# Loading x ahead of the weights, and a last product with buffers of its own, in a four-layer attention kernel

## The chip, the cores and the metric

The kernel runs on one core of one Trainium2 chip. The metric is the device time of one execution in microseconds (us), as the median of several runs. The engines are named as in the profile: PE (TensorE, matrix products), DVE (VectorE), ACT (ScalarE), POOL (GpSimd) and SP (SyncE, which here only issues transfers).

## What is computed

A residual stream x of 2048 tokens by 640 features passes through four layers, A, B, A, B. Each layer adds its result for the layer-normalised x.

```python
x = A_x
x = x + _A_ref(_layernorm(x), A_wq, A_wk, A_wv, A_wo, A_beta)
x = x + _B_ref(_layernorm(x), B_mem0, B_Wq, B_Wk, B_Wv, B_Wo, B_seg_len)
x = x + _A_ref(_layernorm(x), A_wq, A_wk, A_wv, A_wo, A_beta)
x = x + _B_ref(_layernorm(x), B_mem0, B_Wq, B_Wk, B_Wv, B_Wo, B_seg_len)
```

Layer A has 32 heads of 20 features. It cuts the tokens into four segments of 512; within a segment it computes causal softmax attention, and mixes it by a gate per head with a linear-attention read of a state that the earlier segments have filled:

```python
for s in range(4):
    p = softmax(qs @ ks.T * scale + mask);  a_dot = p @ vs
    a_mem = (phi(qs) @ M) / (phi(qs) @ z + 1e-6)
    o = g * a_mem + (1 - g) * a_dot
    M += phi(ks).T @ vs;  z += phi(ks).sum()
return concat(o) @ wo
```

Layer B has 32 heads of 128 features and is recurrent. It makes 64 steps over segments of 32 tokens. In each step 8 memory rows stand ahead of the 32 tokens; the attention's result for these 8 rows is the memory of the next step, and that for the 32 tokens is the output.

```python
for s in range(64):
    h = concat([mem, x[32 * s:32 * s + 32]])
    o = attention(h @ Wq, h @ Wk, h @ Wv, mask) @ Wo
    mem, out[s] = o[:8], o[8:]
```

## The kernel before, in words

The residual stream lies in DRAM (`xres`, float32, with a bfloat16 copy). A layer reads its rows from there and writes them back. Only the first layer reads the input, and only the last writes the output.

**Layer A** (`layer_A`, L161). Each segment is four tiles of 128 tokens. `seg_load` (L220) loads an x tile, `a_xt`, from a pool of two buffers and makes its layernorm `a_xn` at once (two statistics steps, an aggregation and an addition on DVE, a power on POOL, the normalisation on DVE; L80 to L87). `seg_tr` (L229) transposes `a_xn` on PE into PSUM and ACT copies it to `a_xnT` (L237), a pool of two buffers. When all four tiles are there, `proj_q` (L276, `a_QP`) and `proj_k` (L295, `a_KP`) multiply with weights of a group of four heads; eight groups make a segment, so a layer has 32 groups. The rest of a group is scores, row maxima on DVE (L375), exponentials on ACT (L410), products, and the state's update. `out_stage_b` adds the output product to x (L261). A's instructions are given to the framework's scheduler, which decides the order on each engine from dependencies, program order and its own estimate of times. Its PSUM is a pool of three double banks (`psx`, banks 0 to 5) and one of two banks (`pg`, banks 6 and 7), which the transposes and `a_QP` use.

`load_A_weights` (L141) is called after the second x tile of a layer. The first time wq and wk go into a staging place (a corner of B's resident weights), loaded at the very beginning of the program (L1090), and from there DVE copies the 20 columns of each head to a place of 32 (L148), whose other 12 POOL sets to zero (L147). The padded form is kept in DRAM, and the second A layer loads it directly (L150).

**Layer B** (`layer_B`, L543). Here the order on each of PE, ACT, DVE and POOL is the program's own (`_OrdNC`); SP's transfers are not tied. A step gives `b_OPS`, the output of 24 tokens and the memory rows. The product for the last 8 tokens of four consecutive steps is deferred: their attention results are collected in `b_OTdef` and multiplied during the next four steps (`od_chunk`, a quarter at a time) into the PSUM tile `b_OPSd`. `od_begin` (L849) starts one, and `od_end` (L845) adds it to `b_XOd`, the tile with the matching rows of x, and stores it. The next product then needs `b_XOd` loaded anew (`tail_dma`, L822) and the PSUM tile back. After step 63 the deferred product of steps 60 to 63 is still to be done, all four quarters in a row (L1072 to L1074). B's PSUM is a pool of five banks and one with a bank each for the tags `tail`, `ops` and `opsd`.

Of the kernel before, what the change touches and what calls it, by code (L numbers as in the profile page):

```python
# [18 lines left out]
F32 = mybir.dt.float32  # L19
BF16 = mybir.dt.bfloat16  # L20
# [8 lines left out]
D = 640  # L29
# [111 lines left out]
def load_A_weights(nc, W, A_wq, A_wk, A_wv, A_wo, padded, stage):  # L141

    first = not padded
    for nm, src, pad in (("wq", A_wq, W.wq), ("wk", A_wk, W.wk)):
        if first:
            raw = stage[nm]
            nc.gpsimd.memset(pad[:, :, :, 20:32], 0.0)  # L147
            nc.vector.tensor_copy(pad[:, :, :, 0:20], raw.rearrange("p c (h d) -> p c h d", d=20))  # L148
        else:
            nc.sync.dma_start(pad[:].rearrange("p c h s -> p (c h s)"), padded[nm])  # L150
    nc.sync.dma_start(W.wv[:], A_wv.rearrange("(c p) n -> p c n", p=128))
    nc.sync.dma_start(W.wo[:], A_wo.rearrange("(c p) n -> p c n", p=128))
# [8 lines left out]
def layer_A(nc, tc, C, W, x_src, x_dst, src_is_bf16, nseg=4, out_bf16=False, xb_dst=None, load_w=None, side_loads=None):  # L161
    SC = 1.0 / math.sqrt(20.0)
    nc_raw = nc
    if A_ORDERED:
        nc = _OrdNC(tc, nc_raw, engines=ORDER_ENGINES)
# [3 lines left out]
    with ExitStack() as ctx:  # L169
# [7 lines left out]
        pxT = pool("a_xnT", 2)  # L177
        pxt = pool("a_xt", 2)
# [7 lines left out]
        wk = pool("a_wk", 2)  # L186
# [31 lines left out]
        SEG = {}  # L218

        def seg_load(n_, tt):  # L220
            d = SEG.setdefault(n_, {"xn": [None] * 4, "oT": [None] * 4, "xr": [None] * 4})
            r0 = n_ * 512 + tt * 128
            xt = pxt.tile([128, 2 * D] if src_is_bf16 else [128, D], BF16 if src_is_bf16 else F32, name="a_xt")
            nc.sync.dma_start(xt[:, 0:D], x_src[r0:r0 + 128, :])
            xn = pxn.tile([128, D], BF16, name="a_xn")
            layernorm_tile(nc, sml, C, xt[:, 0:D], xn[:], "a_ln")
            d["xn"][tt] = xn
# [219 lines left out]

        for tt in range(4):
            seg_load(0, tt)
            if tt == 1:  # L450
                load_w()
            seg_tr(0, tt)
        proj_q(0)
        proj_k(0)
# [1 line left out]
        for g in range(NGR + 2):  # L456
            n, G = divmod(g, 8)
            for half in range(2):
                p = 2 * g + half
                for r in range(3):  # L460
                    if g < NGR:
                        s_round(p, r)
                    if 0 <= p - 3 < 2 * NGR:
                        t_round(p - 3, r)
                    k = (half, r)
                    if k == (0, 0) and g + 1 < NGR:
                        proj_q(g + 1)
                    if k == (0, 1):
                        if 0 <= g - 1 < NGR:
                            q_with_max(g - 1)  # L470
                        if n >= 1 and 2 <= G <= 5 and n <= nseg:
                            out_stage_a(n - 1, G - 2)
                        if n + 1 < nseg and G in (0, 1, 6):
                            seg_load(n + 1, min(G, 2))
                            seg_tr(n + 1, min(G, 2))
                    if k == (0, 2) and g + 1 < NGR:
                        proj_k(g + 1)
                    if k == (1, 0) and g < NGR:
                        proj_v(g)
                    if k == (1, 1):  # L480
                        if 0 <= g - 2 < NGR:
                            pv(g - 2)
                        if g < NGR:
                            phi_k(g)
                    if k == (1, 2):
                        if 0 <= g - 2 < NGR:
                            norm(g - 2)
                        if g < NGR:
                            state(g)
                        if n >= 1 and 2 <= G <= 5 and n <= nseg:  # L490
                            out_stage_b(n - 1, G - 2)
                        if n + 1 < nseg and G == 6:
                            seg_load(n + 1, 3)
                            seg_tr(n + 1, 3)
            if g < NGR:
                negmax_rows(g)
            if side_loads is not None and n == 0:
                if G == 0:
                    build_gates(nc, st, W, side_loads[1])
                side_loads[0](G, GS[g]["kT"])  # L500
# [42 lines left out]
def layer_B(nc, tc, C, W, x_src, xb_src, x_dst, mem0, B_Wv, B_Wo, nsteps=64, out_bf16=False, tag=""):  # L543
# [7 lines left out]
    with ExitStack() as ctx:  # L551
# [291 lines left out]
                    od["n"] = k + 1  # L843

        def od_end():  # L845
            x_out(od["ps"], XOd, lambda xo: tail_dma(od["s0"], True, xo), "d")
            od.clear()

        def od_begin(s0):  # L849
            od.update(s0=s0, n=0, ps=po.tile([128, 320], F32, name="b_OPSd", tag="opsd"))  # L850

        def ln_g(s):
            return 2 * (s // 8) + 4 + (s % 8 == 5)
# [4 lines left out]
        for s in range(nsteps):  # L858
# [200 lines left out]
                vtail_evac(unit[0], unit[1], vps, "act")  # L1059
            if od and od["n"] == 4:  # L1060
                od_end()
                tail_dma(s - 3, False, XOd)
                od_begin(s - 3)
            elif s == 3:
                tail_dma(0, False, XOd)
                od_begin(0)
            x_out(ops, XO, store_head(s), "")
            nc.gpsimd.tensor_copy(OTdef[(s // 4) % 2][:, :, 8 * (s % 4):8 * (s % 4) + 8], OTsb[:].rearrange("p (h c) -> p h c", c=40)[:, :, 0:8])
            if ln_xt_due(s + 1):
# [7 lines left out]
def full_kernel(tc, A_x, A_wq, A_wk, A_wv, A_wo, A_beta, B_x, B_mem0, B_Wq, B_Wk, B_Wv, B_Wo, B_seg_len, out, layers="ABAB"):  # L1077
    nc = tc.nc
    with ExitStack() as ctx:
        C, WA = alloc_consts(tc, ctx)  # L1080
        xin = A_x.rearrange("b s d -> (b s) d")
        xout = out.rearrange("b s d -> (b s) d")
        mem0 = B_mem0.rearrange("b t d -> (b t) d")
        X = tc.dram_tile([S_TOK, D], F32, name="xres")
        Xb = tc.dram_tile([S_TOK, D], BF16, name="xres_bf")
        WB = alloc_B_resident(tc, ctx)
        padded = {}
        stage = {nm: t_[:, NCH - 1, 0:NCH * D].rearrange("p (c n) -> p c n", c=NCH) for nm, t_ in (("wq", WB.wq), ("wk", WB.wk))}
        for nm, src in (("wq", A_wq), ("wk", A_wk)):
            nc.sync.dma_start(stage[nm], src.rearrange("(c p) n -> p c n", p=128))  # L1090
        build_consts(nc, tc, C)
        nl = len(layers)
        assert layers[0] == "A" and layers[-1] == "B"
        for li, L in enumerate(layers):
            lastl = (li == nl - 1)
            if L == "A":
                first = li == 0

                def side(G, after):
                    load_B_resident(nc, WB, B_Wq, B_Wk, G, after)  # L1100
# [66 lines left out]
```

## Time and profile before

| what | us |
|---|---|
| median of three runs | 2835.52 |
| lowest and highest | 2830.86, 2836.12 |
| the profiled execution | 2836.99 |
| its span, first to last instruction | 2835.3 |
| PE busy | 2667.9 (94%) |
| DVE busy | 1676.5 (59%) |
| ACT busy | 1567.3 (55%) |
| POOL busy | 702.8 (25%) |

A row of the timeline gives the start in us from the beginning of the span, the busy time in us, engine, line, operation, output and inputs, and how many instructions are merged (x5). In brackets stands how long the engine was idle before it and what ended that. SPq and ACTq are the queues on which SP and ACT issue transfers; the time there is that of the issue. The chain of waits follows the program back from its last instruction and names at each step what released it. The granted clock is that of TensorE, 1.00 being full speed. Nearly all helpers of layer B record their operations under one line (L105), so its groups are told apart by tile names.

### The profile page before, as it was taken

Reading aid. Unit: us, or ns where it says so; the run is one execution under the profiler, and the core shown is the slowest. Engines: PE = TensorE matmul, PEld = TensorE weight load, DVE = VectorE, ACT = ScalarE, POOL = GpSimd, SP = SyncE. Lnnn points to the kernel's source line nnn. Section 1 sums busy time; section 2 is a strip of 40 time slices with the busy share of each in tenths; the row PEclk is TensorE's granted clock in tenths of the full one; section 3 lists DMA queues with packets and bytes.
Section 4 is the critical chain, followed back from the end, with each engine's and each line's share of the span. In section 5 each row is a group of like instructions: output and inputs, shape, how many; then the busy total and the mean of one; then the engine's idle time right before and its main releaser. Section 6 shows DMA issues by size and latency. Waiting matters only on the chain.

```text
span 2835.3 us, 147285 instructions
## 1 busy us (share of the span) xinstructions
PE 2667.9 (94%) x65736; PEld 1703.8 (60%) x65736; DVE 1676.5 (59%) x4554; ACT 1567.3 (55%) x3516; POOL 702.8 (25%) x1634
## 2 busy tenths in 40 slices
PE   5899998999999999999979999889999999999998
PEld 2455555666666666666635555556666666666665
DVE  5778864555555555555568878545555555555554
ACT  3777773555555555544448777545555555555443
POOL 3456651111111111111135666411111111111110
PEclk9999999999999999999989999899999999999999
DMA  6110135212221222121130111531211111211110
GB/s 215 53 43 23 39 127 134 44 40 47 44 44 42 43 46 45 41 41 31 31 114 20 57 48 34 174 94 41 43 39 41 41 41 42 43 40 38 39 26 20
DMA packets 322956, 156.54 MB, mean 55 GB/s; under 512 B 245776, under 2 KB 311056, under 8 KB 319248
## 3 DMA queue, kind: packets, MB, share of 16 engines
q1 hardware_dynamic: 320880, 136.63, 19.1%
q8 instruction: 514, 8.42, 1.3%
q10 hardware_dynamic: 1440, 10.49, 1.0%
q14 instruction: 122, 1.00, 0.1%
HBM read 95.65 MB, written 51.38 MB: 52 GB/s over the span
## 4 chain that ended last, share of the span: by engine, by line
PE 54%; DVE 4%; ACT 3%; DMA 2%; issue 1%; POOL 1%; SPq 0%; ACTq 0%; DVEq 0%; POOLq 0%
PE b_OPS L105 7%; PE b_tail L105 4%; PE b_Ka L105 4%; PE b_Qa L105 4%; PE b_Kb L105 4%; PE b_Qb L105 4%; PE b_Va L105 3%; PE b_Vb L105 3%; PE b_SP L105 3%; PE b_OTP L105 2%; PE b_PTP L105 2%; PE b_vtail L105 2%; PE b_OPSd L105 2%; DVE a_nm L375 2%; PE a_QP L276 1%
## 5 line engine op out<-in xcount | busy, mean ns | idle before, releaser
L105 PEld LDWEIGHTS <-b_HX 128*32 128x32 bf16 x15360 | 435.9, 97 | 338.7 <-issue 16.5
L375 DVE TENSOR_REDUCE a_nm<-a_S 128x2 f32<-128x1024 f32 (+3 forms) x512 | 403.7, 811 | 95.1 <-PE a_T L407 71.3
L105 POOL TENSOR_TENSOR b_Pm<-b_E,b_rs 128x96 bf16<-128x96 bf16 x128 | 63.5, 496 | 1446.1 <-ACT b_Vth L105 1082.8
L410 ACT ACTIVATE a_PT<-a_T 128x1024 bf16<-128x1024 f32 (+1 forms) x384 | 340.7, 891 | 51.7 <-PE a_T L407 46.8
L105 PE MATMUL b_OPS<-b_wo,b_OTsb 128*32 128x320 bf16 x8192 | 309.9, 301 | 10.3 <-issue 7.3
L105 PEld LDWEIGHTS <-b_OTsb 128*32 128x32 bf16 x8192 | 201.5, 97 | 97.7 <-DVE b_OTsb L105 25.9
L412 POOL TENSOR_SCALAR_AFFINE_SELECT a_PT<-a_PT 128x256 bf16<-128x256 bf16 (+1 forms) x384 | 198.6, 520 | 235.2 <-ACT a_PT L410 234.0
L105 DVE CAST b_HX<-b_MT 128x8 bf16<-128x8 f32 x372 | 63.7, 172 | 278.5 <-PE b_MT L105 273.4
L105 ACT CAST b_msb<-b_OPS 128x64 bf16<-128x64 f32 x378 | 69.3, 256 | 238.0 <-PE b_OPS L105 238.0
L105 ACT CAST b_kq<-b_Kb 128x512 bf16<-128x512 f32 x128 | 75.0, 586 | 202.4 <-PE b_Kb L105 202.4
L105 DVE COPY b_KT<-b_TPak 128x128 bf16<-128x128 bf16 x128 | 28.8, 225 | 227.2 <-PE b_TPak L105 227.2
L105 PE MATMUL b_Va<-b_wv,b_HX 128*32 128x512 bf16 x2520 | 160.7, 380 | 0.0
L105 PE MATMUL b_Vb<-b_wv,b_HX 128*32 128x512 bf16 x2520 | 160.0, 379 | 0.0
L407 PE MATMUL a_T<-a_q,a_kT 32*128 32x512 bf16 (+3 forms) x1024 | 139.6, 307 | 21.4 <-DVE a_nm L375 14.9
L105 PE MATMUL b_Ka<-b_wk,b_HX 128*32 128x512 bf16 x2520 | 159.0, 379 | 0.0
L105 PE MATMUL b_Kb<-b_wk,b_HX 128*32 128x512 bf16 x2520 | 158.9, 379 | 0.0
L105 PE MATMUL b_Qa<-b_wq,b_HX 128*32 128x512 bf16 x2520 | 158.9, 379 | 0.0
L105 PE MATMUL b_Qb<-b_wq,b_HX 128*32 128x512 bf16 x2520 | 158.9, 379 | 0.0
L105 PEld LDWEIGHTS <-b_kq 128*128 128x128 bf16 x2080 | 116.9, 98 | 69.0 <-ACT b_kq L105 54.8
L105 DVE TENSOR_SCALAR b_kq<-b_Qa 128x512 bf16<-128x512 f32 x128 | 88.5, 692 | 116.7 <-PE b_Qa L105 114.0
L105 DVE CAST b_OTsb<-b_OTP 128x160 bf16<-128x160 f32 (+1 forms) x384 | 122.5, 373 | 40.5 <-PE b_OTP L105 40.3
L105 PE MATMUL b_vtail<-b_wv,b_TX 128*32 128x256 bf16 x2880 | 138.9, 271 | 8.0 <-issue 4.8
(196 smaller groups left out, 5745.1 us busy)
## 6 DMA issues: line engine op xcount, KB each, us to landing
b_QKd<-b_tu SPq DMA_DIRECT2D x128, 128.0 KB
b_tl<-b_QKd SPq DMA_DIRECT2D x128, 128.0 KB
b_wv<-in_B_Wv_dram SPq DMA_DIRECT2D x10, 1024.0 KB
b_wo<-in_B_Wo_dram SPq DMA_DIRECT2D x16, 640.0 KB
b_VTd<-b_vt SPq DMA_DIRECT2D x256, 32.0 KB
b_Vth<-b_VTd SPq DMA_DIRECT2D x512, 16.0 KB
b_XO<-xres SPq DMA_DIRECT2D x256, 30.0 KB
b_wk<-in_B_Wk_dram ACTq DMA_DIRECT2D x5, 1024.0 KB
```

Source lines behind the costliest of these rows:

```text
L105: r = f(*a, **k)
L276: nc.tensor.matmul(QP[:], lhsT=wqG[:, c, :], rhs=xnT[:, c, :], start=(c == 0), stop=(c == NCH - 1))
L375: nc.vector.tensor_reduce(out=nm[:, qc, 2 * pr:2 * pr + 2], in_=X[:, :, o:o + w_], axis=AX.X, op=ALU.max, negate=True)
L407: nc.tensor.matmul(Y[:, e, o:o + w_], lhsT=kT[rows, 128 * kc:128 * kc + 128], rhs=q2[rows, 128 * kc:512], start=True, stop=True, tile_posi ...
L410: nc.scalar.activation(out=PT[:, :, b:b + width], in_=Y[:, :, 0:width], func=ACT.Exp, scale=SC)
L412: nc.gpsimd.affine_select(out=dv, in_=dv, pattern=[[0, 2], [0, diag], [1, 128]], compare_op=ALU.is_ge, fill=0.0, base=0, channel_multiplie ...
```

## The change

Four things change.

- In segment 0 of each A layer the loads of all four x tiles come first in the program, then the weights, then norm and transposes of the four tiles. `seg_load` is split into `seg_load` and `seg_norm`. Tiles 2 and 3 do not use the two buffers of `a_xt` but one buffer of the `xnT` pool, as the tile `a_xt2`.
- In the first A layer the staging loads of wq and wk move from the program's beginning into `load_A_weights`, behind the four x loads.
- The copies from the staging place to the padded weights go from DVE to ACT.
- The last deferred product of each B layer gets the PSUM bank of the tag `tail`, and an x tile of its own, `b_XOe`, in the place of B's layernorm input `xt`. It is loaded in step 62, so that neither the bank of the product before nor its `b_XOd` has to come free.

```diff
 def load_A_weights(...):
     first = not padded
+    if first:
+        for nm, src in (("wq", A_wq), ("wk", A_wk)):
+            nc.sync.dma_start(stage[nm], src.rearrange("(c p) n -> p c n", p=128))
...
             nc.gpsimd.memset(pad[:, :, :, 20:32], 0.0)
-            nc.vector.tensor_copy(pad[:, :, :, 0:20], raw.rearrange("p c (h d) -> p c h d", d=20))
+            nc.scalar.copy(pad[:, :, :, 0:20], raw.rearrange("p c (h d) -> p c h d", d=20))
...
         def seg_load(n_, tt):
...
-            xt = pxt.tile([128, 2 * D] if src_is_bf16 else [128, D], BF16 if src_is_bf16 else F32, name="a_xt")
+            if n_ == 0 and tt >= 2:
+                if tt == 2:
+                    d["xt2"] = pxT.tile([128, 2, 2 * D] if src_is_bf16 else [128, 2, D], BF16 if src_is_bf16 else F32, name="a_xt2", tag="xnT")
+                xt = d["xt2"][:, tt - 2, :]
+            else:
+                xt = pxt.tile([128, 2 * D] if src_is_bf16 else [128, D], BF16 if src_is_bf16 else F32, name="a_xt")[:]
             nc.sync.dma_start(xt[:, 0:D], x_src[r0:r0 + 128, :])
+            d["xt"][tt] = xt
+
+        def seg_norm(n_, tt):
+            d = SEG[n_]
+            xt = d["xt"][tt]
             xn = pxn.tile([128, D], BF16, name="a_xn")
             layernorm_tile(nc, sml, C, xt[:, 0:D], xn[:], "a_ln")
...
         for tt in range(4):
             seg_load(0, tt)
-            if tt == 1:
-                load_w()
+        load_w()
+        for tt in range(4):
+            seg_norm(0, tt)
             seg_tr(0, tt)
...
         def od_end():
-            x_out(od["ps"], XOd, lambda xo: tail_dma(od["s0"], True, xo), "d")
+            x_out(od["ps"], od["xo"], lambda xo: tail_dma(od["s0"], True, xo), "d")
             od.clear()

-        def od_begin(s0):
-            od.update(s0=s0, n=0, ps=po.tile([128, 320], F32, name="b_OPSd", tag="opsd"))
+        def od_begin(s0, xo, tag="opsd"):
+            od.update(s0=s0, n=0, xo=xo, ps=po.tile([128, 320], F32, name="b_OPSd", tag=tag))
...
                 od_end()
-                tail_dma(s - 3, False, XOd)
-                od_begin(s - 3)
+                if last:
+                    od_begin(s - 3, XOe, "tail")
+                else:
+                    tail_dma(s - 3, False, XOd)
+                    od_begin(s - 3, XOd)
             elif s == 3:
                 tail_dma(0, False, XOd)
-                od_begin(0)
+                od_begin(0, XOd)
+            if s == nsteps - 2:
+                XOe = bx.tile([64, 320], F32, name="b_XOe", tag="xt")
+                tail_dma(nsteps - 4, False, XOe)
             x_out(ops, XO, store_head(s), "")
...
         stage = {...}
-        for nm, src in (("wq", A_wq), ("wk", A_wk)):
-            nc.sync.dma_start(stage[nm], src.rearrange("(c p) n -> p c n", p=128))
         build_consts(nc, tc, C)
```

In the segments after the first, `seg_norm` is called right behind `seg_load`, as both were one before.

More of the change, by code (lines that the diff above doesn't have):

```diff
@@ L220, in seg_load @@
         def seg_load(n_, tt):
-            d = SEG.setdefault(n_, {"xn": [None] * 4, "oT": [None] * 4, "xr": [None] * 4})
+            d = SEG.setdefault(n_, {"xt": [None] * 4, "xn": [None] * 4, "oT": [None] * 4, "xr": [None] * 4})
             r0 = n_ * 512 + tt * 128
-            xt = pxt.tile([128, 2 * D] if src_is_bf16 else [128, D], BF16 if src_is_bf16 else F32, name="a_xt")
+            if n_ == 0 and tt >= 2:
[4 more added lines that the diff above has]
+                xt = pxt.tile([128, 2 * D] if src_is_bf16 else [128, D], BF16 if src_is_bf16 else F32, name="a_xt")[:]
             nc.sync.dma_start(xt[:, 0:D], x_src[r0:r0 + 128, :])
+            d["xt"][tt] = xt
+        def seg_norm(n_, tt):
+            d = SEG[n_]
+            xt = d["xt"][tt]
             xn = pxn.tile([128, D], BF16, name="a_xn")
@@ L474, in layer_A @@
                             seg_load(n + 1, min(G, 2))
+                            seg_norm(n + 1, min(G, 2))
                             seg_tr(n + 1, min(G, 2))
@@ L493, in layer_A @@
                             seg_load(n + 1, 3)
+                            seg_norm(n + 1, 3)
                             seg_tr(n + 1, 3)
```

## The prediction

> **What bounds the kernel now.** I read the page first: engine shares, the slices, and the chain that ended last.
>
> ```profile
> PE   5899998999999999999979999889999999999998
> ...
> PE 54%; DVE 4%; ACT 3%; DMA 2%; issue 1%; POOL 1%; SPq 0%; ACTq 0%; DVEq 0%; POOLq 0%
> ```
>
> TensorE is busy nearly everywhere and carries the chain. The weak slices are the first, those around the middle and the last: the start of layer A, the change from the first B to the second A, and the end. The edit is at exactly these places, so I read the timeline of each, beginning with the start.
>
> ```profile
> 1.86 1.21 SPq L224 DMA_DIRECT2D a_xt<-in_A_x_dram  x2
> ...
> 8.32 0.49 DVE L80 BATCH_NORM_STATS2 a_ln_st<-a_xt 128x6 f32<-128x320 bf16 x1 [5.35 <-DMA a_xt<-in_A_x_dram]
> ...
> 9.12 0.21 DVE L61 CAST c_identb<-c_identf 128x128 bf16<-128x128 f32 x1
> ...
> 10.06 0.14 DVE L72 TENSOR_REDUCE c_krow<-c_krows 128x1 f32<-128x8 f32 x1
> ...
> 10.58 0.97 DVE L148 COPY a_wq_pad<-b_wq 128x3200 bf16<-128x3200 bf16 x1
> 10.86 2.34 POOL L147 MEMSET a_wq_pad<- 128x1920 bf16 x1
> ...
> 11.63 1.75 DVE L87 TENSOR_SCALAR a_xn<-a_xt,a_ln_mv,a_ln_rstd 128x640 bf16<-128x640 bf16 x1
> ...
> 16.61 3.42 SPq L224 DMA_DIRECT2D a_xt<-in_A_x_dram  x2
> ...
> 22.04 0.49 DVE L80 BATCH_NORM_STATS2 a_ln_st<-a_xt 128x6 f32<-128x320 bf16 x1 [1.57 <-DMA a_xt<-in_A_x_dram]
> ...
> 25.78 2.29 PE L276 MATMUL a_QP<-a_xnT,a_wq_pad 128*128 128x512 bf16 x5 [0.78 <-ACT a_xnT L237]
> ```
>
> The x tiles stand in SP's queue behind the two staged weights (L1090), so the first layernorm starts at 8.32. Tile 3 is issued only when tile 1 has given its buffer back (16.61) and is read at 22.04. The first real product, a_QP, waits for the last transposed tile until 25.78.
>
> The second A, in the chain of waits in order of time:
>
> ```profile
> 1414.88 3.04 DMA a_xt<-xres
> ...
> 1423.94 2.30 DMA xres<-b_XOd
> ...
> 1427.05 2.97 DMA b_XOd<-xres
> ...
> 1430.65 0.50 DVE b_XOd L105
> ...
> 1433.08 6.26 DMA a_xt<-xres
> ...
> 1443.82 0.73 PE a_tps L236 x5
> 1444.58 0.70 ACT a_xnT L237
> 1445.32 2.29 PE a_QP L276 x5
> ```
>
> Two x tiles come at once. The other two are issued on SP behind B's last two stores: the one of b_XOd must land before b_XOd can be loaded again for the last deferred product, then come the add, its store, and at 1433.08 x tiles 2 and 3. DMA was done with the weights and nearly free from 1424 on, as the windows show (columns: stretch, its length, five engines' busy time, granted clock, DMA share, GB/s):
>
> ```profile
> 1422.00:1424.00 2.00, 0.00 (x0) 0.00 (x0) 1.55 (x4) 0.00 (x0) 0.35 (x1) 0.97 1.01 425
> 1424.00:1426.00 2.00, 1.94 (x32) 1.39 (x36) 0.95 (x3) 0.00 (x0) 0.00 (x0) 0.50 0.25 76
> ```
>
> The end has the same loop through b_XOd:
>
> ```profile
> 2825.50 2.36 PE L105 MATMUL b_OPSd<-b_wo,b_OTdef 128*32 128x320 bf16 x64 [1.20 <-DVE b_xnbd L105]
> ...
> 2826.82 1.34 SPq L830 DMA_DIRECT2D b_XOd<-xres  x2
> 2828.26 1.68 SPq L819 DMA_DIRECT2D out_dram<-b_xnb  x2
> ...
> 2830.37 0.48 DVE L105 TENSOR_TENSOR b_XOd<-b_OPSd,b_XOd 64x320 f32<-64x320 f32 x1 [3.97 <-DMA b_XOd<-xres]
> ...
> 2831.41 1.37 SPq L828 DMA_DIRECT2D out_dram<-b_xnbd  x2
> ```
>
> **The start, part by part.** SP now issues four x tiles, then wq and wk. The sizes of one transfer in the second A and in the first, and the rate before the change:
>
> ```profile
> a_xt<-xres SPq DMA_DIRECT2D x8, 320.0 KB
> ```
>
> ```profile
> a_xt<-in_A_x_dram SPq DMA_DIRECT2D x9, 160.0 KB
> ...
> b_wq<-in_A_wq_dram SPq DMA_DIRECT2D x1, 800.0 KB
> ```
>
> ```profile
> 4.00:6.00 2.00, 0.00 (x0) 0.00 (x0) 0.00 (x0) 0.00 (x0) 0.92 (x2) 1.00 1.06 381
> ```
>
> Until 8.32, two weights and two x tiles came in (1,920 KB, 1.97 MB): 5.2 us at 381 GB/s, so 3.1 us are issue and latency. In the new order x0 lands at 3.5, x3 (0.66 MB) at 4.8, wq at 7.0, wk at 9.1. The norms go at DVE's pace, for one undisturbed tile (first and last of its six rows, one of them POOL's):
>
> ```profile
> 17.18 0.48 DVE L80 BATCH_NORM_STATS2 a_ln_st<-a_xt 128x6 f32<-128x320 bf16 x1
> ...
> 19.23 0.45 DVE L87 TENSOR_SCALAR a_xn<-a_xt,a_ln_mv,a_ln_rstd 128x640 bf16<-128x640 bf16 x1 [0.74 <-POOL a_ln_rstd L86]
> ```
>
> That is 2.50 us, of which DVE waits 0.74 for POOL, a gap that the next tile's statistics can fill: four tiles are 4 x 1.76 = 7.0, plus one gap. DVE also has about 0.9 of small constant copies (five, from 9.12 to 10.06). POOL's memset of the weights' padding beside the norms stretches a_xn from 0.45 to 1.75; with two memsets 2.6. So the last a_xn ends near 3.5 + 7.0 + 0.7 + 0.9 + 2.6 = 14.7; its transposes and the 0.7 evacuation make about 16.1, and 13.5 without the stretching. I take 15.5, as part of the padding may be filled before the norms. Gain 25.8 - 15.5 = 10.3, between 7.8 (a_QP at 18, if POOL's small steps queue behind the memsets too) and 12.3.
>
> The Trainium skill speaks against this part: SBUF — State Buffer, "Who interferes with whom", says that VectorE in a two-port mode and GpSimd lock each other out of a port pair for a whole instruction. The trace agrees in kind (1.75 beside a 2.34 memset, 0.45 alone); by the rule in full, two memsets of 2.34 could cost 4.7 and not 2.6, so a_QP would come 2.1 later, inside the bounds above.
>
> The two padding copies leave DVE (0.97 each) for ScalarE, where no such copy is seen. Its nearest rows give the price:
>
> ```profile
> 52.71 1.01 ACT L410 ACTIVATE a_PT<-a_T 128x1024 bf16<-128x1024 f32 x1
> ...
> 55.48 0.60 ACT L410 ACTIVATE a_PT<-a_T 128x512 bf16<-128x512 f32 x1 [0.19 <-PE a_T L407]
> ```
>
> 0.41 us per 512 elements makes 2.75 us for 3,200; bounds are 0.97, as on DVE, and twice 2.75. This is a new wait: ACT stands at wq until 7.0, then copies to 9.8, wk to 12.6. Queued behind it are the evacuations of the transposes, whose two PSUM buffers TensorE needs back. Even with both copies ahead of all four evacuations (0.7 each) the last ends at 15.4, no later than DVE's chain; so I cost it at nothing, and at up to 3 if copies take twice as long. The order of the staging loads matters to nobody else.
>
> **The second A.** x tiles 2 and 3 take the second buffer of the transposed tile. It lies like wq's within the old b_wv, and is free when the last b_Vb ends; so all four follow at 1414.88. The first two took 3.04; 0.66 MB more at 425 GB/s add 1.5: landed by 1419.5. wq and wk, which kept DMA busy to about 1424.3, land by 1425.8, before they are needed.
>
> ```profile
> 1423.95 1.01 DVE L105 TENSOR_TENSOR b_XO<-b_OPS,b_XO 64x320 f32<-64x320 f32 x2
> 1424.06 3.92 PE L105 MATMUL b_OPSd<-b_wo,b_OTdef 128*32 128x320 bf16 x64 [2.98 <-DVE b_XOd L105]
> ```
>
> The last b_OPSd no longer waits 2.98 for its bank and starts near 1421.1. It takes 2.4 to 3.9 and leaves TensorE by 1425. A's transposes use the two banks of b_OPS and b_OPSd: free when b_XO is added at 1424.96. From there transposes of tiles 0 and 1, and on DVE what is left of norms 2 and 3 (up to 2 x 1.9, float input) and the new b_XOe add (1.01): 1424.96 + 4.8 + 0.7 puts the last a_xn at 1430.5 if nothing of it was done before, and near 1427.2 if the statistics fit in earlier gaps. Transposes and evacuation add 1.4, so a_QP starts between 1428.6 and 1432. A memset of A's state lies over the place of b_XOe and must wait for its store; if it is ordered ahead of a norm on DVE, up to 2 us more. I take 1431: gain 14.3, from 11.3 to 16.7. Two loads for b_XOe move to step 62, ahead of SP's store and next b_XO load: 1.34 us of issue in a queue whose next load is first read in the following step's add; at nothing, under that step's products, or 1.34 if that cover were gone.
>
> **The end.** No load stands between the product and the add. b_OPSd starts at 2824.3, ends at 2826.7 (1.6 later at the cold pace of 3.92); the add takes two steps of 0.5, to 2827.7. On SP the store of b_xnb moves up to 2826.8 and takes 1.68, so the last store starts at 2828.45 instead of 2831.41: gain 2.9, at least 1.3.
>
> Sum: 10.3 + 14.3 + 2.9 = 27.5, from 20.4 to 32. The profiled execution took 2836.99 (span 2835.3 and 1.7 around it), 1.5 above the median of the three runs. 2836.99 - 27.5 = 2809.5; against the median 2835.52 it is **2808.0**, 2803 to 2815.
>
> **The rivals.** Everything behind the two starts is supposed to move up unchanged. Layer A's order is not written by hand, though, but made by a scheduler from its own estimate of times, which the edit alters. How much an order can be worth, the same text shows in both A layers (last two numbers: first and last start):
>
> ```profile
> L261 DVE TENSOR_TENSOR a_xnew<-a_YP,a_xr x32: 476/480/493, 164.8 to 431.6; 128x320 f32<-128x320 f32 x32
> L261 DVE TENSOR_TENSOR a_xr<-a_YP,a_xr x32: 476/480/492, 1564.6 to 1831.7; 128x320 f32<-128x320 f32 x32
> ```
>
> From a_QP to the last output add the first takes 405.8 and the second 386.4: 19.4 apart.
>
> (1) Slower: both A layers come out in an order worse by 19.4 each. 2808 + 38.8 = 2846.8. It decides from 13.8 per layer on, 0.43 us for each of its 32 head groups. For it speaks the spread; against it, that no instruction behind the starts changes its place in the text, and that part of the 19.4 is the loading of B's weights in the first A.
>
> (2) Only the second A falls into the first one's order: 2827.4.
>
> (3) The first A gains the second's order: 2788.6.
>
> (4) The weights become the last to land. In the second A, a_wv already goes out behind B's stores:
>
> ```profile
> 1428.57 0.52 SPq L151 DMA_DIRECT2D a_wv<-in_A_wv_dram  x1
> ```
>
> If wq and wk do too, 2.62 MB and 3.0 of latency put them at 1437.7, and a_KP, due at 1433, 5 later; with the copies on ScalarE at their dear end 2.5 more at the start: 2815.5. Against it: they stand ahead of a_wv in the text and wait for nothing later than the x tiles do.
>
> (5) The clock stays full through both starts: a_QP (2.29 cold) and the equal a_KP run in half, 2.3 per start, 4.6 more in all: 2803.4. The row at 1424 shows clock 0.50 after an idle stretch. The Trainium skill, TensorE: Matmul & The Clock Gate, "What's actually happening", has the clock halved after about 3.4 us of idleness. The trace agrees (2.98 idle ahead of the product at 1424.06, then 0.50). Against it: transposes with gaps are little work.
>
> **How the numbers follow.** Forecast 0.50, (1) 0.12, (2) 0.12, (3) 0.08, (4) 0.10, (5) 0.08. The range leaves out (1) and (3), 0.20 together: 2798, 5 below the forecast's own low end for a first A that improves in part, to 2828, which holds (2). A measurement of this kernel tells about 0.2%, 5.7 us, from no change: faster is below 2829.8. All but (1) lie there, and (2) only with two thirds of its chance: 0.84 faster, 0.04 the same, 0.12 slower.
>
> **What would show it.** Right: four a_xt issues in a row at the start and after b_Vb; a_QP near 15.5, and in the second A near 1420.7 (1445.3 less both gains); no DMA wait ahead of the last add; the last store 3.9 before the end of the span, as now. Wrong: a DVE or ACT wait for weights ahead of a_QP, or an A layer whose stretch from a_QP to its last add is not within 5 us of 405.8 and 386.4.

## The result, and the profile after

| what | before | after |
|---|---|---|
| median of nine runs each, us | 2831.18 | 2815.97 |
| lowest and highest | 2826.18, 2838.94 | 2811.19, 2823.91 |
| the profiled execution | 2836.99 | 2814.01 |

The ratio is 0.9946 (95% interval 0.9933 to 0.996): faster by 15.2 us, between 11 and 19, where 27.5 were forecast. The kernel before ran again for this, so its median is no longer the 2835.52 that the forecast stands on. A second set of runs of the changed kernel, six beside eleven of the kernel before, gave 0.9946 again (0.9929 to 0.9962).

The first start, in the timeline of the changed kernel:

```profile
0.81 1.81 SPq L232 DMA_DIRECT2D a_xt<-in_A_x_dram  x4
...
7.34 1.70 POOL L150 MEMSET a_wq_pad<- 128x1920 bf16 x1 [2.43 <-DVE c_krow L72]
8.98 1.70 POOL L150 MEMSET a_wk_pad<- 128x1920 bf16 x1
...
9.69 1.28 ACT L151 ACT_TABLE_LOAD   x1 [9.69 <-DMA b_wq<-in_A_wq_dram]
...
10.98 2.86 ACT L151 COPY a_wq_pad<-b_wq 128x3200 bf16<-128x3200 bf16 x1
11.25 0.97 DVE L87 TENSOR_SCALAR a_xn<-a_xt,a_ln_mv,a_ln_rstd 128x640 bf16<-128x640 bf16 x2 [3.96 <-POOL a_ln_rstd L86]
...
13.26 0.96 DVE L87 TENSOR_SCALAR a_xn<-a_xt,a_ln_mv,a_ln_rstd 128x640 bf16<-128x640 bf16 x2 [0.61 <-POOL a_ln_rstd L86]
13.74 2.85 ACT L151 COPY a_wk_pad<-b_wk 128x3200 bf16<-128x3200 bf16 x1
...
16.50 1.28 ACT L250 COPY a_xnT<-a_tps 128x640 bf16<-128x640 bf16 x2
...
17.97 1.29 ACT L250 COPY a_xnT<-a_tps 128x640 bf16<-128x640 bf16 x2
...
19.30 2.29 PE L289 MATMUL a_QP<-a_xnT,a_wq_pad 128*128 128x512 bf16 x5 [0.78 <-ACT a_xnT L250]
```

Four x loads go out in a row, as forecast. Then read ACT alone: it stands until wq lands at 9.69, loads a table for 1.28, copies 2.86 and 2.85, and only then evacuates the transposes. VectorE's last norm is done at 14.2. So a_QP starts at 19.30, 6.5 earlier than before and not 10.3.

The second start, again the timeline:

```profile
1405.71 1.76 SPq L232 DMA_DIRECT2D a_xt<-xres  x4
...
1414.26 1.53 PE L105 MATMUL b_OPSd<-b_wo,b_OTdef 128*32 128x320 bf16 x38 [1.38 <-issue]
...
1419.98 0.55 POOL L86 TENSOR_TENSOR a_ln_rstd<-a_ln_rstd,c_mhalf 128x1 f32<-128x1 f32 x1
...
1420.56 0.61 DVE L87 TENSOR_SCALAR a_xn<-a_xt,a_ln_mv,a_ln_rstd 128x640 bf16<-128x640 f32 x1 [2.14 <-POOL a_ln_rstd L86]
1420.59 1.16 SPq L232 DMA_DIRECT2D a_xt<-xres  x2
...
1422.72 0.58 PE L289 MATMUL a_QP<-a_xnT,a_wq_pad 128*128 128x512 bf16 x1 [0.78 <-ACT a_xnT L250]
```

All four tiles follow the last b_Vb, no wait for a DMA stands ahead of the last b_OPSd, and a_QP comes 17.0 after the x loads where it came 30.4 after (1414.88 to 1445.32). What is last now is the fourth norm: its power runs on POOL only at 1419.98, behind memsets of A's state, the last of which starts at 1419.47.

The end, with the adds and stores of the last deferred product:

```profile
2805.53 0.48 DVE L105 TENSOR_TENSOR b_XOe<-b_OPSd,b_XOe 64x320 f32<-64x320 f32 x1
2805.89 1.66 SPq L835 DMA_DIRECT2D out_dram<-b_xnb  x2
2807.41 0.49 DVE L105 TENSOR_TENSOR b_xnbd<-b_OPSd,b_XOe 64x320 bf16<-64x320 f32 x1 [1.40 <-DMA out_dram<-b_xnbd]
2807.93 1.37 SPq L844 DMA_DIRECT2D out_dram<-b_xnbd  x2
```

The 3.97 wait for b_XOd is gone. A smaller one has come: the second half waits 1.40 for the tile b_xnbd, which the product before still stores. And the A layers (last number: start of the last output add):

```profile
L274 DVE TENSOR_TENSOR a_xnew<-a_YP,a_xr x32: 477/480/493, 158.5 to 425.2; 128x320 f32<-128x320 f32 x32
L274 DVE TENSOR_TENSOR a_xr<-a_YP,a_xr x32: 477/480/493, 1547.6 to 1815.1; 128x320 f32<-128x320 f32 x32
```

From a_QP the first takes 405.9 (405.8 before). The second takes 392.4 and not 386.4: 6.0 are given back behind the start.

### The profile page after: what moved, and what is told of

It is laid out like the page before. It is cut to its first block, busy times and chain, and to the rows that moved or that the text cites. A ratio compares the mean times of both kernels' runs of the same rounds, so it can differ in the third digit from the quotient of the medians.

```text
span 2812.2 us, 147216 instructions
## 1 busy us (share of the span) xinstructions
PE 2657.2 (94%) x65671; PEld 1696.4 (60%) x65736; DVE 1672.3 (59%) x4552; ACT 1571.8 (56%) x3518; POOL 699.2 (25%) x1634
## 3 DMA queue, kind: packets, MB, share of 16 engines
q1 hardware_dynamic: 320880, 136.63, 19.2%
## 4 chain that ended last, share of the span: by engine, by line
PE 79%; DVE 8%; ACT 5%; DMA 3%; issue 2%; POOL 2%; SPq 0%; ACTq 0%; DVEq 0%; POOLq 0%
PE b_OPS L105 10%; PE b_tail L105 5%; PE b_Ka L105 5%; PE b_Qb L105 5%; PE b_Qa L105 5%; PE b_Kb L105 5%; PE b_Va L105 5%; PE b_Vb L105 4%; PE b_SP L105 4%; DVE a_nm L388 4%; PE b_OTP L105 3%; PE b_PTP L105 3%; PE b_OPSd L105 3%; PE b_vtail L105 3%; PE a_QP L289 2%; PE a_KP L308 2%
## 5 line engine op out<-in xcount | busy, mean ns | idle before, releaser
L420 PE MATMUL a_T<-a_q,a_kT 32*128 32x512 bf16 (+3 forms) x1024 | 139.4, 306 | 20.7 <-DVE a_nm L388 15.1
L379 PE MATMUL a_S<-c_negu,c_identb 128*128 128x128 bf16 (+1 forms) x768 | 124.7, 242 | 23.3 <-DVE a_nm L388 14.7
```

The source lines that it names most:

```text
L379: nc.tensor.matmul(X[:, e, m0:m1], lhsT=C.identb[:], rhs=C.negu[:, 0:(m1 - m0) // 128, :].rearrange("p a k -> p (a k)"), start=True, stop= ...
L420: nc.tensor.matmul(Y[:, e, o:o + w_], lhsT=kT[rows, 128 * kc:128 * kc + 128], rhs=q2[rows, 128 * kc:512], start=True, stop=True, tile_posi ...
```

## The experiments

The stretches of all profiles are read as these were, in us. "First body" and "second body" go from a layer's first a_QP to the end of its last output add (0.5 more than to its start), "gap" from the end of the first B's last b_Vb to the second A's a_QP. The clock is the granted one from 26 to 76 us. The ratio is to the kernel before, in runs on the same chip.

| kernel | first a_QP | first body | gap | second body | clock | ratio (95%) |
|---|---|---|---|---|---|---|
| before | 25.8 | 406.3 | 30.5 | 386.9 | 0.83 | 1 |
| changed | 19.3 | 406.4 | 17.0 | 392.8 | 0.83 | 0.9946 (0.9933 to 0.996) |
| changed, again | 17.9 | 407.0 | 17.7 | 392.5 | 0.80 | 0.9946 (0.9929 to 0.9962) |
| tail alone | 25.8 | 417.5 | 30.7 | 384.7 | 0.74 | 0.9985 (0.9971 to 1.0) |
| loads alone | 19.3 | 404.3 | 20.5 | 387.5 | 0.83 | 0.9951 (0.9933 to 0.9969) |
| copies on DVE | 19.0 | 402.9 | 17.7 | 392.2 | 0.83 | 0.9941 (0.9919 to 0.9963) |
| early table | 20.7 | 404.4 | 17.8 | 392.6 | 0.83 | 0.9955 (0.9941 to 0.9969) |
| DVE copies, gate late | 17.7 | 403.5 | 16.7 | 392.8 | 0.86 | one run |
| ordered start | 14.6 | 405.8 | 18.4 | 394.1 | 0.84 | 0.9936 (0.9918 to 0.9953) |
| ordered, zeros on ACT | 15.6 | 404.6 | 17.3 | 391.1 | 0.81 | 0.9929 (0.9916 to 0.9942) |
| shifted norms | 19.7 | 402.6 | 18.5 | 388.9 | 0.83 | 0.9917 (0.9899 to 0.9935) |
| ordered and shifted | 15.1 | 407.7 | 16.9 | 387.8 | 0.76 | 0.9924 (0.9909 to 0.9939) |
| ordered, ACT zeros, shifted | 14.8 | 411.8 | 17.6 | 386.1 | 0.73 | 0.9951 (0.9939 to 0.9963) |
| the same, shifted in second A only | 15.0 | 416.5 | 17.7 | 384.7 | 0.64 | 0.9918 (0.9899 to 0.9937) |

**The changed kernel again.** 

> The changed kernel once more, unaltered, for a second profile and as the pair of the three others. If the differences that the profiles show between kernels with the same code in the B layers (982.8, 980.0, 980.5, 982.1 and 976.6 us from the first A layer's last output add to the last value product of the first B layer) are of one execution, the same stretch lands anywhere from 976 to 983 here, while the first a_QP (19.3 +- 0.3), the stretch from the last value product to the second layer's a_QP (17.0 +- 0.7) and the second A body (392.8 +- 1) repeat. Ratio to before 0.9946 +- 0.0015. Rival: the starts and the A body vary as much as B does, and then no term of the sum can be read from one profile.

Measured: the first B (last add to last b_Vb) took 978.4, inside 976 to 983; the gap and second body repeat. The first a_QP came 1.4 earlier than forecast, since wq landed at 8.29. Between these two profiles the first start, the gap and the second body differ by at most 1.4. The first B can't be read from one profile: over all fourteen it spreads from 975.8 to 982.8, with the code of B's steps the same. Nor can the first body: the tail alone leaves the first A's code as it was before, and its profile has 417.5 where the kernel before has 406.3. The profiled executions of the kernel before and of the changed one differ by 23.0, more than the medians; 7.1 of it lies in the two B parts, the second taken up to the last work on the deferred product before the last (2823.84 and 2802.86).

**The two parts alone.** The tail on the kernel before, and the changed kernel without it:

```diff
-                if last:
-                    od_begin(s - 3, XOe, "tail")
-                else:
-                    tail_dma(s - 3, False, XOd)
-                    od_begin(s - 3, XOd)
+                tail_dma(s - 3, False, XOd)
+                od_begin(s - 3, XOd)
...
-            if s == nsteps - 2:
-                XOe = bx.tile([64, 320], F32, name="b_XOe", tag="xt")
-                tail_dma(nsteps - 4, False, XOe)
```

This diff takes the tail out of the changed kernel.

> The kernel before with only the last part of the change: the last deferred product of each B has a bank and an x tile of its own. Theory (two causes that mostly add): from the last b_Vb to the second A's a_QP 27 instead of 30.5 us, since x tiles 2 and 3 still follow the last store and two weights; at the end of the program 2.5 less. In sum about 6 us less than before, ratio near 0.998. Rival (two locks in a row): the part at the second A brings nothing alone, only the end's 2.5, ratio 0.999.

> The kernel after without its last part: the last deferred product of B uses the tag opsd and b_XOd again. From the end of the last b_Vb of the first B to the second A's a_QP it takes 30.5 us before and 17.0 after. Theory (two causes that mostly add): the early x tiles alone bring it to about 19.2, because the transposes of tiles 1 to 3 still wait for the reloaded b_XOd; the end of the program is as before. In sum some 12 us less than before, ratio near 0.9958. Rival (two locks in a row): without the product's own buffers the x tiles bring little, it stays above 26, ratio near 0.998.

Measured: alone, the tail leaves the gap at 30.7, so its rival held: without the early loads, x tiles 2 and 3 still land last there. The loads alone bring the gap from 30.5 to 20.5, near their theory's 19.2. The tail takes 3 us more off the gap, but the second body is 392 to 393 with both and 387.5 with the loads alone: gap and body together are 408.0 without the tail and 409.8 and 410.2 with it. So in these profiles, one of the loads alone and two with both, the tail bought nothing in the second A; its gain is at the end of the program.

**What held the first start.** One line back:

```diff
-            nc.scalar.copy(pad[:, :, :, 0:20], raw.rearrange("p c (h d) -> p c h d", d=20))
+            nc.vector.tensor_copy(pad[:, :, :, 0:20], raw.rearrange("p c (h d) -> p c h d", d=20))
```

> The kernel after, with the two padding copies of wq and wk back on VectorE. Theory (ScalarE is the new bound of the first start): after the change both copies (2.86 us each) and a table load (1.28) stand on ScalarE ahead of all four evacuations, so a_QP starts at 19.30 instead of about 16. With the copies on VectorE (0.97 each) it starts near 17, and the rest follows: about 2 us less than the kernel after, ratio to before near 0.994. Rival (landing): wq lands only at 9.7 and wk later, whoever copies; a_QP stays at 19.3 within 0.5 and the time is that of the kernel after.

```profile
9.06 1.70 POOL L150 MEMSET a_wk_pad<- 128x1920 bf16 x1
9.29 2.32 DVE L151 COPY a_wq_pad<-b_wq 128x3200 bf16<-128x3200 bf16 x1 [1.93 <-DMA b_wq<-in_A_wq_dram]
...
16.06 0.23 ACT L135 ACTIVATE a_beta_e<-a_beta_bf 128x32 f32<-128x32 bf16 x1 [13.97 <-DMA a_beta_bf<-in_A_beta_dram]
...
18.99 2.29 PE L289 MATMUL a_QP<-a_xnT,a_wq_pad 128*128 128x512 bf16 x5 [0.78 <-ACT a_xnT L250]
```

These rows are that kernel's timeline. a_QP stayed at 19.0, as the rival had it, but not for its reason: wq had landed by 9.29. ACT's queue was free of copies, but the exponential of layer A's gate, which is made from the input beta, now stood in it ahead of the evacuations and waited for beta until 16.06. The next kernel loads the table early:

```diff
+        warm = C.pool.tile([128, 1], F32, name="c_warm")
+        nc.vector.memset(warm[:], 0.0)
+        nc.scalar.activation(out=warm[:], in_=warm[:], func=ACT.Exp)
```

> The kernel after, with a one-column exponential on ScalarE at the very start, so that the table load no longer stands behind the wait for wq. Theory (ScalarE's chain bounds the first start): a_QP moves up by the table load's 1.28, from 19.3 to 18.0. Rivals: if VectorE's and GpSimd's norm chain or the landing of the weights bounds it, a_QP stays at 19.3 within 0.3. In the total 1.3 us is hardly to be told from nothing.

Measured: the load ran at 0.81 and the wq copy began at 9.37, but a_QP came at 20.7. In its timeline:

```profile
16.43 0.18 DVE L136 TENSOR_SCALAR a_beta_e<-a_beta_e 128x32 f32<-128x32 f32 x1 [3.26 <-ACT a_beta_e L135]
...
16.89 0.55 POOL L86 TENSOR_TENSOR a_ln_rstd<-a_ln_rstd,c_mhalf 128x1 f32<-128x1 f32 x1 [4.33 <-DVE a_ln_rstd L85]
```

VectorE now had the gate's steps ahead of the last two norms and stood behind beta for 3.26. So a third kernel had the copies on VectorE and put the gate's exponential behind the evacuation of the first a_kT, by an edge that only orders the program and makes no engine wait:

```diff
...
-    nc.scalar.activation(out=e[:], in_=bb[:], func=ACT.Exp, scale=-1.0)
+    op = nc.scalar.activation(out=e[:], in_=bb[:], func=ACT.Exp, scale=-1.0)
+    tc.add_manual_dep(op.ins, last.ins.name, mybir.DependencyInfo(mybir.DependencyClass.NoSync, mybir.DependencyReason.SCHED_ONLY), reason="order")
...
```

> The changed kernel with the two padding copies back on VectorE and the gate's exponential behind the first a_kT on ScalarE; the order of norms and copies is the scheduler's. If ScalarE's queue alone held a_QP (copies in the one kernel, beta's landing at 16.06 in the other), the evacuations now follow the transposes from 14.3 on and a_QP starts at 17 (16.5 to 17.5), held by VectorE: wq's landing at 9.3, two copies, four a_xn. Rival: a_QP stays at 18.5 or above, and the bound is neither queue.

Measured: 17.65, just above 16.5 to 17.5. The evacuations now follow the transposes without a wait for weights or beta: ACT's queue had held a_QP, by its copies in one kernel and by beta in the other. But the gain is small, 1.65 against the changed kernel's first profile and 0.3 against its second, in one run: VectorE now had the copies, 2.01 and 2.32 long beside the memsets, ahead of its norms, and the last norm ended at 16.0.

**The order of the start.** Copies on VectorE and GpSimd's zeroing both behind the four norms, by such edges (`after`), and the gate late as above:

```diff
+def pad_A_weights(nc, tc, W, stage, last):
...
+        after(nc.gpsimd.memset(pad[:, :, :, 20:32], 0.0))
+        after(nc.vector.tensor_copy(pad[:, :, :, 0:20], stage[nm].rearrange("p c (h d) -> p c h d", d=20)))
```

> The changed kernel with three things altered in the first start, by order alone: the copies to the padded weights are back on VectorE, they and GpSimd's zeroing of the padding stand behind the four norms of segment 0, and the gate's exponential on ScalarE, which needs beta's late load, stands behind the first a_kT. Theory (what held a_QP at 19.3 was ScalarE's queue: wq landing at 9.7, two copies of 2.86 and 2.85, four evacuations of 0.65 behind them, and with the copies on VectorE beta's landing at 16.1): nothing of this is left ahead of the evacuations, they run as the norms come (5.5 to 9), the wq copy runs from its landing near 9.5 to 11.8, and a_QP starts at 11.8 to 13, 6 to 7.5 us earlier; ratio near 0.992. Rival (the layer's start is bounded by a stream behind a_QP: wk's copy, wv's landing, segment 1's loads): a_QP does move but the first A body grows by as much, and the ratio stays within 0.001 of 0.9946. Rival 2: a_QP stays above 16, held by something else (the landing of the x tiles).

```profile
7.28 0.79 DVE L87 TENSOR_SCALAR a_xn<-a_xt,a_ln_mv,a_ln_rstd 128x640 bf16<-128x640 bf16 x2
...
9.12 3.94 DVE L87 TENSOR_SCALAR a_xn<-a_xt,a_ln_mv,a_ln_rstd 128x640 bf16<-128x640 bf16 x2 [0.61 <-PE a_tps L254]
9.54 1.70 POOL L159 MEMSET a_wq_pad<- 128x1920 bf16 x1
...
11.18 1.70 POOL L159 MEMSET a_wk_pad<- 128x1920 bf16 x1
...
14.61 2.29 PE L294 MATMUL a_QP<-a_xnT,a_wq_pad 128*128 128x512 bf16 x5 [0.78 <-ACT a_xnT L255]
```

a_QP moved to 14.61, the best of the study, but not to 13. Two a_xn take 0.79; the next two took 3.94, while both memsets ran from 9.54 to 12.88: the edges order GpSimd's queue, so the memsets came behind its last power there, but not behind VectorE's last a_xn. The first body did not grow (405.8), and the ratio, 0.9936, lies between the theory's 0.992 and the rival's 0.9946 and decides for neither. Next, the same with the zeros on ACT, copied from a tile that is zero:

```diff
+def zero_pads(nc, W, zero):
+    for pad in (W.wq, W.wk):
+        nc.scalar.copy(pad[:, :, :, 20:32], zero.unsqueeze(1).unsqueeze(1).to_broadcast([128, NCH, 32, 12]))
```

> The kernel with the altered order of the first start, and one thing more: the zeros of the two paddings are written by ScalarE in its idle time after 2.4 us, not by GpSimd behind the norms. Theory (in that kernel the third and fourth a_xn took 3.94 us together, where two take 0.79 to 0.97, because the last of them stood while GpSimd's two memsets of 1.70 ran from 9.54 to 12.88): the four a_xn end near 10, the wq copy near 11, and a_QP starts at 11.6 to 12.4 instead of 14.61. Rival (the last a_xn waited for something else, or the wq copy for wq's landing near 12): a_QP stays within 0.7 of 14.6, or at 13.5. Time: 2.5 us less than the ordered kernel if the fill behind a_QP keeps them, the same if segment 1's loads, read at 16.46 there, or the landing of wv bound it.

```profile
9.43 1.79 ACT L170 CAST a_wq_pad<-a_MZ 128x1920 bf16<-128x1920 f32 x1
9.80 0.97 DVE L87 TENSOR_SCALAR a_xn<-a_xt,a_ln_mv,a_ln_rstd 128x640 bf16<-128x640 bf16 x2 [0.61 <-PE a_tps L260]
10.68 0.99 DVE L159 COPY a_wq_pad<-b_wq 128x3200 bf16<-128x3200 bf16 x1
11.13 1.78 ACT L170 CAST a_wk_pad<-a_MZ 128x1920 bf16<-128x1920 f32 x1
...
15.62 2.29 PE L300 MATMUL a_QP<-a_xnT,a_wq_pad 128*128 128x512 bf16 x5 [0.78 <-ACT a_xnT L261]
```

The memsets were the cause: the two a_xn are back at 0.97, and the wq copy ends near 11.7. But a_QP came at 15.62, a miss of both forecasts: ACT's queue waited until 8.14, by the profile for VectorE's last step on the constants (c_krow), loaded its table, and then wrote the zeros ahead of the evacuations. The ratio fell to 0.9929; against 0.9946 for the changed kernel the intervals overlap.

**What the second A gives back.** Segment 1's first three tiles are handled one group later:

```diff
-                        if n + 1 < nseg and G in (0, 1, 6):
-                            seg_load(n + 1, min(G, 2))
...
+                        early = (1, 2, 6) if n == 0 else (0, 1, 6)
+                        if n + 1 < nseg and G in early:
+                            seg_load(n + 1, early.index(G))
```

> The changed kernel with one thing moved: the first three tiles of segment 1 are loaded, normed and transposed in groups 1, 2 and 6 of segment 0 instead of 0, 1 and 6. Theory (what the second A layer gives back is the norm of segment 1's first two tiles, which the idle time ahead of the layer covered before the change and which now stands between the first row maxima on VectorE, with its transposes ahead of the second a_KP on TensorE): the second A body, from a_QP to the end of the last output add, goes from 392.8 back to 387 to 389, the first A body doesn't grow, and the ratio to before is near 0.993. Rival (the fill is slow because TensorE's granted clock is low after the shorter start, mean 0.59, 0.70, 0.50 in its first three stretches of 6 us): the body stays at 391 or above, ratio near 0.9946. A third way: group 1 or 2 pays what group 0 saved, body 391 to 394.

The windows behind a_QP (stretch, length, five engines' busy time, granted clock, DMA share, GB/s), of the changed kernel and then of this one:

```profile
1422.72:1428.72 6.00, 5.77 (x16) 2.01 (x16) 0.04 (x1) 1.27 (x2) 0.00 (x0) 0.59 1.06 388
1428.72:1434.72 6.00, 3.39 (x23) 1.12 (x22) 5.84 (x8) 0.58 (x1) 0.00 (x0) 0.70 0.06 23
1434.72:1440.72 6.00, 3.04 (x13) 1.59 (x15) 4.23 (x12) 0.69 (x1) 1.61 (x4) 0.50 0.18 52
```

```profile
1422.23:1428.23 6.00, 6.00 (x19) 2.11 (x20) 0.33 (x1) 1.27 (x2) 0.00 (x0) 0.64 1.02 376
1428.23:1434.23 6.00, 4.83 (x51) 2.44 (x47) 5.67 (x8) 2.14 (x4) 0.14 (x1) 0.93 0.02 5
1434.23:1440.23 6.00, 6.00 (x28) 2.26 (x26) 4.20 (x8) 1.01 (x2) 1.58 (x5) 0.50 0.00 0
```

In the second and third stretch of the changed kernel TensorE is idle for nearly half the time, and VectorE has 5.84 and 4.23 us of work. The reason is in the timelines, first of the kernel before:

```profile
1444.99 0.49 DVE L80 BATCH_NORM_STATS2 a_ln_st<-a_xt 128x6 f32<-128x320 f32 x1 [1.22 <-DMA a_xt<-xres]
...
1451.75 4.15 DVE L375 TENSOR_REDUCE a_nm<-a_S 128x2 f32<-128x1024 f32 x5 [1.57 <-PE a_S L372]
```

Then of the changed one:

```profile
1428.68 2.09 DVE L388 TENSOR_REDUCE a_nm<-a_S 128x2 f32<-128x1024 f32 x2 [7.51 <-PE a_S L385]
...
1438.42 0.72 PE L249 MATMUL a_tps<-c_identb,a_xn 128*128 128x128 bf16 x5 [2.35 <-DVE a_xn L87]
...
1438.93 1.49 PE L308 MATMUL a_KP<-a_xnT,a_wk_pad 128*128 128x512 bf16 x3
```

Before, segment 1's first norm began at 1444.99, just ahead of a_QP (1445.32), and VectorE had done two norms before the first row maxima. In the changed kernel the second a_KP stands behind transposes of segment 1, and these behind a norm that VectorE reaches only after the first row maxima, at 1435.56. With the shift the second body is 388.9, and in all four shifted kernels 384.7 to 388.9, against 391.1 to 394.1 in the seven that have early loads, the tail and no shift. So the place of segment 1's norms is the cause. The low clock remains in part (0.64, 0.93, 0.50) and is no bar to the gain; as it rose in the second stretch, how much of the gain is the clock's own is not separated. What put the norms behind the row maxima is not shown either. VectorE had been idle for 7.51 before these, but segment 1's tiles were issued only at 1420.59, behind wv and wo, and the transfer engines were full (DMA share 1.06) up to 1428.7. The tiles may have landed too late for the idle time, whatever the order.

> Both alterations of the two kernels before in one: the order of the first start, and segment 1's norms in groups 1, 2 and 6. If both theories hold and the gains add, the first a_QP is at 11.8 to 13, the second A body 387 to 389, and the ratio to before near 0.9905 (some 11 us below the changed kernel). If the gain in the first start is given back in its fill, this shift should return part of it in the first A layer too, and the ratio is 0.991 to 0.993. If neither holds, 0.9946.

> The same with segment 1's first norms in groups 1, 2 and 6. a_QP as in the kernel beside it. If the first A layer's fill is bounded by segment 1's norms the first A layer ends 2 to 4 us earlier than in the kernel beside it, and the second A body is 387 to 389; ratio to before near 0.990. If the first start's gain is lost behind a_QP in any case: 0.9917 to 0.9924, as the two kernels with this shift had it before.

> The kernel with the altered order of the first start and ScalarE's zeros, and segment 1's first norms in groups 1, 2 and 6 in the second A layer alone. Theory (the shift returns what the second A's fill lost, 4 to 5 us, and costs the first A layer as much after an early start: its body was 411.8 us with the shift and 404.6 without): first a_QP at 15.6, first A body 404 to 406, second A body 386 to 389, ratio to before near 0.991 (some 5 us below the same kernel without the shift, 10 below the changed one). Rival (the body of the first A layer with the shift, 411.8, was one execution's, not the shift's, as 402.6 with the shift and the later start suggests): the second A body still falls to 386 to 389, but the ratio stays at 0.9929 +- 0.001 because the median differs from its profile by as much.

Measured: the second body fell each time, to 387.8, 386.1 and 384.7. The first body did not stay: it was 407.7, 411.8 and, without the shift in the first A, 416.5, where 404 to 406 had been expected. The first kernel's ratio, 0.9924, lies in its middle forecast, though its a_QP came at 15.1. The second kernel missed both of its forecasts: its first A ended 6.3 later than in the kernel beside it, not 2 to 4 earlier, and its ratio is 0.9951. The last one's interval holds both the theory's 0.991 and the rival's 0.9929. Whether the shift makes the first body long after an early start stays open. The last profile speaks against it, but that execution took 2805.15, 5.8 above the kernel's median; and for it speaks that the ratios without and with the shift in the first A, 0.9918 and 0.9951, have intervals that just don't overlap. What goes with a long first body in the profiles is a low granted clock in the 100 us from 26 on. Here are the windows from 26 to 126, first of the changed kernel, then of the tail alone (417.5), then of the last kernel (416.5):

```profile
26.00:76.00 50.00, 37.53 (x388) 19.43 (x389) 31.52 (x58) 22.87 (x38) 15.02 (x41) 0.83 0.53 186
76.00:126.00 50.00, 43.96 (x554) 23.48 (x559) 37.16 (x70) 36.88 (x59) 25.81 (x60) 0.97 0.13 45
```

```profile
26.00:76.00 50.00, 36.08 (x297) 17.08 (x299) 28.36 (x56) 18.52 (x29) 12.95 (x36) 0.74 0.48 172
76.00:126.00 50.00, 44.77 (x492) 22.71 (x494) 27.39 (x46) 29.97 (x46) 19.05 (x46) 0.75 0.17 60
```

```profile
26.00:76.00 50.00, 38.91 (x316) 18.87 (x318) 25.69 (x49) 20.63 (x32) 15.06 (x41) 0.64 0.50 187
76.00:126.00 50.00, 44.45 (x568) 23.92 (x568) 34.13 (x63) 34.63 (x54) 22.38 (x51) 0.86 0.15 50
```

From 26 to 76 TensorE is busy for 36 to 39 us in all three, yet the last kernel, whose a_QP came 4.3 earlier, gets 316 products done where the changed one gets 388. The tail alone starts when the kernel before does, and gets 297 and 492 done in the two windows where that kernel gets 318 and 592. For the tail alone this is the one execution's: its first start is that of the kernel before, and the profiled execution, 2833.28, was the slowest of twelve (median 2819.82). Whether an earlier start also draws a lower clock stays open; of the kernels with a_QP below 16, four of five had 0.81 or less.

The shifted kernel and the last one are the fastest ratios here, 0.9917 and 0.9918. In the same set of runs the shifted kernel took 2805.19 against 2811.13 for the changed one, 5.9 less, with intervals that overlap by 0.0006.

## Why the prediction was right in sign, and half in size

Faster, and inside the range, but the sum was 27.5. The sum's own bounds, a gain of 20.4 to 32 and a time of 2803 to 2815, were missed by 15.2 and 2815.97. The range held because it had been widened to 2828 for rival (2), a dearer second A, which came in part and by another way; that is luck more than reckoning. Term by term, from the two profiles of the changed kernel against that of before:

| term | forecast | changed | again |
|---|---|---|---|
| first start | 10.3 | 6.5 | 7.9 |
| second start | 14.3 | 13.4 | 12.8 |
| end | 2.9 | 2.1 | 2.1 |
| first body | 0 | -0.1 | -0.7 |
| second body | 0 | -5.9 | -5.6 |
| sum | 27.5 | 16.0 | 16.5 |

The end is read from the last work on the deferred product before the last (2823.84 and 2802.86) to the span's end. The sums lie inside the 11 to 19 measured. The row of the first body says little: as shown above, one execution can have it 11 longer.

**The first start** failed at the step that cost the ACT copies at nothing. The size of a copy was right (2.75 forecast, 2.86), and so was putting both ahead of all evacuations. But the chain was to end at 15.4 and ended at 19.26. Between them are 2.7 for wq's landing, 9.69 for 7.0, and 1.28 for a table load, which in the kernel before no weight's landing held up; the copies and evacuations gave 0.1 back. The Trainium skill, ScalarE: Activation LUTs, "What ACT_TABLE_LOAD costs", has 1283 ns for it; the trace agrees (1.28), and the drain that the section adds for a switch between sets does not show here, as the copy starts at 10.98. wq's landing was worked out as if transfers came in one after another:

```profile
0.00:3.00 3.00, 0.00 (x0) 0.00 (x0) 1.72 (x10) 0.00 (x0) 2.36 (x12) 1.00 0.36 105
3.00:6.00 3.00, 0.00 (x0) 0.00 (x0) 2.90 (x11) 0.00 (x0) 1.91 (x6) 1.00 0.95 239
6.00:9.60 3.60, 1.01 (x6) 0.72 (x6) 1.25 (x7) 0.00 (x0) 2.26 (x2) 1.00 1.04 374
```

By 9.6 some 2.38 MB had moved (length times GB/s), where four x tiles and wq are 1.47 MB: the rest came in beside wq. And the rate from 3 to 6 us was 239, where 381 had been taken.

VectorE's own chain was not late, 14.2 for 14.7, but otherwise than reasoned: no a_xn was stretched. The memsets ran first, and the powers queued behind them on POOL (a_xn waited 3.96), which the forecast had only at the low end of its gain. The ordered kernel then showed what had been left at a part: 3.94 for two a_xn beside two memsets. The Trainium skill, SBUF — State Buffer, "Who interferes with whom", lets the loser block for a whole instruction. The trace agrees and goes further: an a_xn of some 0.45 took 3.43 and ended only behind both memsets, that is through two instructions.

**The second start** was right within 1.5, by its own chain of x loads, though the last step was misnamed: not VectorE's adds and a memset ahead of a norm, but POOL's memsets ahead of a power.

**The end** was right but for the wait of 1.40 on b_xnbd. The last store moved up by 2.5, but the mark of 3.9 from it to the span's end was 4.3 (2807.93 to 2812.2), so 0.4 went again.

**"Everything behind the two starts is supposed to move up unchanged"** failed in the second A: 392.4 for 386.4, beyond the 5 us set as the mark. Rival (1) named the scheduler's order, but as a cost in every group and both layers. It was one place: in the time ahead of the first row maxima, which the change shortened, norms of the next segment had been done. Rival (5) was rightly set low, as a_QP took 2.29 cold in the first A. The idle stretch of 2.98 set beside it is shorter than the time cited there: it bears out the halving, not how long it takes. Rival (4) had a part: wq did not land last, but late. The forecast's mark for being wrong, an ACT wait for weights ahead of a_QP, is just what the profile shows.

## What to carry to other kernels

When a start is shortened, list what ran in it for later stages: those steps don't vanish, they can move behind the new start and into its chain. Cost a moved copy by the whole queue it joins, with the landing that it waits for, a table load, and what stands behind it, and give a transfer's landing the bytes that share the engines with it, not only those ahead. A gain read from two profiles needs the stretches that the edit hardly touches beside it: here the two B parts differed by 7.1 us.

## What the runs showed that was not expected

- The granted clock from 26 to 76 us went from 0.64 to 0.86 between profiles. At 0.80 and above the first A's body took 402.6 to 407.0, below it 407.7 to 417.5, in code that is nearly the same.
- In the ordered kernel two memsets of 1.70 on GpSimd held one VectorE a_xn from near 9.6 to 13.1.
- With the copies on VectorE, a load of 8 KB (beta) that SP issued from 5.74 on was read only at 16.06, behind loads of 800 KB.
